# K stationaries copied by ScalarE, full-height masked sums for the tail, and raised priority for norm and GELU in a fused attention and gating kernel

## The chip, the cores and the metric

The kernel runs on one core of one Trainium2 chip. Five engines work side by side, each with its own queue of instructions in a fixed order: TensorE (PE, matmuls, with its weight loads shown as PEld), VectorE (DVE), ScalarE (ACT), GpSimdE (POOL) and SyncE (SP, which here issues the DMAs). The metric is the device time of one execution in microseconds (us). The kernel before takes 469.25 us (median of 3 runs, 469.03 to 470.44).

## The reference, cut to what matters

```python
scores = q @ k.T / 8                      # 4 batches, 12 heads, 448 positions, head size 64
scores = cap * tanh(scores / cap)
attn = exp(scores - max) / (sum + 1e-9)
x = (attn @ v) as [4, 448, 768]
h = gelu_tanh(x @ w_in)                   # w_in [768, 1024]; u, v = two halves of 512
v = layernorm(v) * g_ln
v = w_sg @ v + b_sg                       # w_sg [448, 448], over positions
out = x + (u * v) @ w_out                 # w_out [512, 768]
```

All of it is float32. To reach that accuracy the kernel splits most matmul operands into a high and a low part of type fp32r and adds three products; the attention sums and `attn @ v` are plain fp32 matmuls.

## The kernel before, in words

Heads are taken in pairs: 4 batches of 6 pairs. The 448 positions of k are 3 chunks of 128 and a tail of 64, so each pair has 4 units: three full ones (both heads, scores 128x896) and one tail unit, in which the 64 tail positions of head 0 and of head 1 share the 128 partitions (128x448). In a unit PE makes the scores (`scores`, L198 for the tail and L212 otherwise), ACT applies tanh (`soft`, L225) and exp (`soft2`, L228), and two units later PE multiplies by v (`av`, L241). The pair's q and k are split ahead of time: `prep_a` makes the high part (L156 or L158) and `prep_b` the low part on DVE (L170). For the tail unit the k columns of both heads must stand as one 128-column stationary with zeros between, the tile `kt`; `prep_b` fills it by two copies of 64x128 elements on POOL (L173).

The row sums of exp (`den`, L261) are matmuls of the probabilities with a 0/1 matrix `ones_sb`, 32 output rows each, four of them side by side in one PSUM tile `den`. In batch 0 all four units of a pair go there; in batches 1 to 3 DVE first adds the pair's units up (`presum`, L297). After the sixth pair `recip` inverts the sums (tile `rds`, L322 last); `norm` spreads them by a matmul (L334), multiplies (L337, DVE), makes the high part (L341, ACT) and the low part (L342 and, for the last 64 columns, L344, DVE). Then the gating network of that batch follows: `hv` (L368), `hu` (L412), `vsg` (L426), `outp` (L455, with the residual added in L460). `gelu2` takes four steps in turn: square (L351, ACT), L352 (DVE), tanh (L356, ACT), L357 (DVE).

These matmuls are written between the attention units of the next batch as fillers, at a rate that the code sets (`filler`); the last batch's network runs alone at the end. Beside batch 0 and 1 the weights are loaded and decoded (`decode`, L560 to L582: 36 pieces, ACT or DVE, then DVE, POOL, DVE, ACT or DVE, POOL; `split_sg`, L545 and L546), three or a few more pieces in flight.

The order on each engine is not that of the text: a scheduler at build time picks, among the instructions that are ready in its own plan, the one of highest priority, which is normally the one written first. Once built, an engine's order is fixed.

Of the kernel before, what the change touches and what calls it, by code (L numbers as in the profile page):

```python
# [7 lines left out]
FP32 = mybir.dt.float32  # L8
# [4 lines left out]
ACTF = mybir.ActivationFunctionType  # L13
ALU = mybir.AluOpType
PSUM = bass.MemoryType.PSUM

GELU_A = 0.044715
GELU_C = 0.7978845608028654
# [36 lines left out]
def kernel(  # L55
# [15 lines left out]
    nc = tc.nc  # L71
    B, NP, _, S = q2.shape
    NC = w_sgT.shape[1]
    FC = S // 128
    TL = S - 128 * FC
# [8 lines left out]
    wp = ctx.enter_context(tc.tile_pool(name="wp", bufs=1))  # L84
# [16 lines left out]
    wsg = [wp.tile([128, NC, S], FP32R, name=f"wsg{s}") for s in range(2)]  # L101
    sel_r = wp.tile([128, NP, 128], FP32R, name="sel_r")
    rds = wp.tile([128, S], FP32R, name="rds")
    ones_sb = wp.tile([128, NP + 31], FP32, name="ones_sb")
    bsg_sb = wp.tile([128, S], FP32, name="bsg_sb")
    g_sb = wp.tile([128, KF], FP32, name="g_sb")
    cap_sb = wp.tile([128, 1], FP32, name="cap_sb")
# [3 lines left out]
    kt = wp.tile([128, 2, 2 * TL], FP32R, name="kt")  # L111

    def f32(ap):
        return ap.bitcast(FP32)
# [4 lines left out]
    def later(d, fn):  # L119
        dq.append((now[0] + d, len(dq), fn))  # L120
# [12 lines left out]
    def two(t):  # L133
        return t.rearrange("p (a s) -> p a s", a=2)
# [31 lines left out]
    def prep_b(P):  # L166
        if P >= NPAIR:
            return
        hl = qks[P]
        nc.vector.tensor_tensor(out=hl[:, 1], in0=two(raws[P]), in1=f32(hl[:, 0]), op=ALU.subtract)  # L170
        for h in range(2):
            rows = slice(64 * h, 64 * h + 64)
            nc.gpsimd.tensor_copy(out=kt[rows, :, TL * h:TL * h + TL], in_=f32(hl)[rows, :, 1, 128 * FC:])  # L173
        raw_s.put(raws.pop(P))

    def prep_first():
# [53 lines left out]
    def heads(src, c):  # L230
        if c:
            return [two(src)[:, h, :] for h in range(2)]
        return [src[TL * h:TL * h + TL, :S] for h in range(2)]
# [18 lines left out]
    def den(b, units):  # L252
        if b not in den_t:
            den_t[b] = ps_d.tile([128, 512], FP32, tag="den", name="den")
            units_in[b] = 0
        t = den_t[b]
        for half, (P, c, src) in enumerate(units):
            for h, pr in enumerate(heads(src, c)):
                j = 2 * half + h
                lo, n = (0, 128) if c else (TL * h, TL)  # L260
                nc.tensor.matmul(  # L261
                    out=t[32 * j:32 * j + 32, :S],
                    lhsT=ones_sb[lo:lo + n, NP - 1 - P % NP:NP + 31 - P % NP], rhs=pr,
                    start=(units_in[b] < 2), stop=(units_in[b] >= NP * (NC - ADDS[b]) - 2),
                    skip_group_check=True)
            units_in[b] += 1
# [34 lines left out]
    def flush():  # L301
        b, units = flushes.pop(0)
        den(b, units)
        for u in units:
            raw_s.put(u[2])
        if units_in[b] == NP * (NC - ADDS[b]):
            boost[0] = True
            recip(b)
            later(READY_LAG, set_ready)
# [15 lines left out]
    def gps():  # L325
        if tail[0]:
            tail[0] += 1
            if tail[0] % 2:
                return ps_s.tile([128, 512], FP32, tag="sc", name="gp")
        return ps_g.tile([128, 512], FP32, tag="g", name="gp")  # L330

    def norm(b, p):
        ps = gps()
        yield 1, lambda: nc.tensor.matmul(  # L334
            out=ps[:, :S], lhsT=sel_r[:, p, :], rhs=rds, start=True, stop=True)
        x = xu[:, xu_t[b, p], :]
        nc.vector.tensor_tensor(out=x, in0=x, in1=ps[:, :S], op=ALU.mult)  # L337

        def split():
            xh[p], xl[p] = r_s.get(), r_s.get()  # L340
            nc.scalar.activation(out=xh[p][:, :S], in_=x, func=ACTF.Copy)  # L341
            nc.vector.tensor_tensor(  # L342
                out=xl[p][:, :S], in0=x, in1=f32(xh[p][:, :S]), op=ALU.subtract)
            nc.vector.tensor_tensor(  # L344
                out=xh[p][:, S:], in0=x[:, S - TL:], in1=f32(xh[p][:, S - TL:S]), op=ALU.subtract)
        split()

    def gelu2(src, n, dst, done):
        sqt = t_s.get()
        sq = sqt[:src.shape[0], :n]  # L350
        nc.scalar.activation(out=sq, in_=src, func=ACTF.Square)  # L351
        nc.vector.scalar_tensor_tensor(  # L352
            out=sq, in0=sq, scalar=1.0 / GELU_A, in1=src, op0=ALU.add, op1=ALU.mult)

        def fin():
            nc.scalar.activation(out=sq, in_=sq, func=ACTF.Tanh, scale=GELU_C * GELU_A)  # L356
            nc.vector.scalar_tensor_tensor(  # L357
                out=dst, in0=sq, scalar=1.0, in1=src, op0=ALU.add, op1=ALU.mult)
            t_s.put(sqt)
            done()  # L360
        later(2, fin)
# [307 lines left out]
    for g in range(NSTEP + LAG + 2):  # L669
        P, c = divmod(g, NC)  # L670
# [13 lines left out]
        if g < NSTEP:  # L684
            soft2(g)
            if c == 0:
                prep_a(P + 1)
            elif c == 1:
                prep_b(P + 1)
                load_pair(P + 2)  # L690
# [92 lines left out]
```

## Time and profile before

| what | value |
|---|---|
| median of 3 runs | 469.25 us |
| the profiled execution | 472.69 us, span 470.9 us |
| PE, DVE, ACT, POOL busy | 93%, 71%, 60%, 20% of the span |
| PE idle | nearly all of it before 182 us and after 405 us |
| mean granted TensorE clock | 0.971 of full speed |

The span runs from the first to the last instruction; about 1.8 us lie around it. A group row gives the source line, engine, operation, the tiles written and read, the shapes and the count, then busy us and mean ns of one. "Released by" or "<-" names what ended an engine's idle time.

### The profile page before, as it was taken

The page shows a single profiled execution, that of the slowest core. Times are in us where ns is not written, and L with a number is a line of the kernel's source. Part 1 is how long each engine was busy: PE and PEld are TensorE (multiplying, and loading weights), DVE is VectorE, ACT ScalarE, POOL GpSimd, SP SyncE. Part 2 cuts the span into 40 slices and gives each one's busy share as a digit, 9 for nine tenths or more (in the row PEclk, how much of TensorE's full clock was granted, in tenths as well). Part 3 has the DMA queues.
Part 4 walks back from the last instruction along what each step waited for, and adds up shares of the span by engine and source line. Part 5 has one row for each costly group of instructions (what it writes and reads, how often), then busy time and mean ns, then how long its engine had stood idle before and what let it go on. Part 6 is the DMA issues. An engine that isn't in the chain of part 4 may idle for free.

```text
span 470.9 us, 5916 instructions
## 1 busy us (share of the span) xinstructions
PE 436.7 (93%) x2097; PEld 272.5 (58%) x2097; DVE 335.7 (71%) x621; ACT 283.1 (60%) x420; POOL 93.0 (20%) x143
## 2 busy tenths in 40 slices
PE   5997769879999869999999999999999999899996
PEld 2332223337466536675656666666666576678985
DVE  4859866987999896588587457388596355687662
ACT  4776688974686665538578756636777760044310
POOL 0436644301425543110110101000111000001000
PEclk9999979989999959999999999999999999999999
DMA  7563334221421231231210220420200001200002
GB/s 222 198 197 125 114 120 131 90 84 45 126 67 45 90 107 61 100 99 42 63 39 25 61 61 1 141 91 10 63 22 2 22 2 39 78 1 0 1 27 90
DMA packets 20717, 34.18 MB, mean 73 GB/s; under 512 B 3024, under 2 KB 12880, under 8 KB 20688
## 3 DMA queue, kind: packets, MB, share of 16 engines
q1 hardware_dynamic: 20688, 33.81, 22.8%
q8 instruction: 16, 0.26, 0.3%
q14 instruction: 13, 0.11, 0.1%
HBM read 28.30 MB, written 5.51 MB: 72 GB/s over the span
## 4 chain that ended last, share of the span: by engine, by line
PE 70%; DVE 18%; DMA 3%; POOL 3%; ACT 3%; issue 3%; SPq 0%; POOLq 0%; DVEq 0%; ACTq 0%
PE pav L241 14%; PE gp L455 13%; PE gp L368 11%; PE gp L412 10%; PE sc L212 8%; PE gp L426 8%; DVE raw L297 3%; PE den L261 3%; PE sc L198 2%; DMA xu<-in_w_in_dram 2%; DVE xu L580 2%; PE gp L334 1%; POOL xu L575 1%; ACT raw L225 1%; DVE hl L170 1%
## 5 line engine op out<-in xcount | busy, mean ns | idle before, releaser
L225 ACT ACTIVATE raw<-sc,qsc 128x896 f32<-128x896 f32 (+1 forms) x96 | 86.6, 906 | 36.9 <-PE sc L212 19.1
L241 PE MATMUL pav<-raw,v 128*64 128x448 f32 x384 | 94.1, 576 | 1.0 <-ACT xu L249 1.0
L228 ACT ACTIVATE raw<-raw,cap_sb 128x896 f32<-128x896 f32 (+1 forms) x96 | 90.1, 944 | 1.3
L212 PE MATMUL sc<-hl 64*128 64x448 f32 x432 | 69.6, 418 | 15.0 <-ACT raw L225 15.0
L297 DVE TENSOR_TENSOR raw<-raw,raw 64x448 f32<-64x448 f32 (+1 forms) x72 | 63.2, 878 | 6.1 <-PE pav L241 5.1
L368 PE MATMUL gp<-win,r 128*128 128x512 f32 x264 | 65.3, 398 | 1.3 <-DVE t L357 1.0
L212 PEld LDWEIGHTS sc<-hl 64*128 64x128 f32 x432 | 38.5, 195 | 47.2 <-ACT raw L225 21.5
L412 PE MATMUL gp<-r,win 128*128 128x448 f32 x288 | 65.1, 373 | 0.1
L455 PE MATMUL gp<-r,wout 128*128 128x448 f32 x288 | 63.6, 372 | 0.0
L412 PEld LDWEIGHTS gp<-r,win 128*128 128x128 f32 x288 | 52.7, 188 | 14.5 <-issue 9.6
L455 PEld LDWEIGHTS gp<-r,wout 128*128 128x128 f32 x288 | 53.1, 188 | 11.3 <-issue 3.8
L368 PEld LDWEIGHTS gp<-win,r 128*128 128x128 f32 x264 | 48.2, 188 | 19.5 <-issue 5.6
L241 PEld LDWEIGHTS pav<-raw,v 128*64 128x64 f32 x384 | 25.6, 141 | 52.4 <-issue 41.5
L173 POOL CAST kt<-hl 64x128 fp32r<-64x128 f32 x46 | 21.9, 476 | 155.6 <-PE sc L198 111.3
L426 PE MATMUL gp<-wsg,r 128*128 128x448 f32 x176 | 41.5, 382 | 3.4 <-DVE u L357 3.4
L426 PEld LDWEIGHTS gp<-wsg,r 128*128 128x128 f32 x176 | 33.0, 193 | 14.1 <-issue 6.5
L352 DVE SCALAR_TENSOR_TENSOR t<-t,gp 128x448 f32<-128x448 f32 (+1 forms) x28 | 18.0, 644 | 20.5 <-ACT t L351 20.3
L170 DVE TENSOR_TENSOR hl<-raw,hl 128x896 fp32r<-128x896 f32 x23 | 25.8, 1122 | 8.3 <-ACT hl L158 8.1
L382 POOL TENSOR_TENSOR rs<-rs,pw 128x1 f32<-128x1 f32 (+1 forms) x16 | 9.6, 600 | 109.2 <-DVE rs L381 109.1
L460 DVE TENSOR_TENSOR xu<-xu,gp 128x448 f32<-128x448 f32 x24 | 14.6, 612 | 22.6 <-PE gp L455 22.4
L356 ACT ACTIVATE t<-t 128x448 f32<-128x448 f32 (+2 forms) x32 | 19.3, 604 | 16.9 <-DVE t L352 16.9
L261 PE MATMUL den<-raw,ones_sb 128*32 128x448 f32 (+1 forms) x168 | 29.4, 589 | 0.0
(81 smaller groups left out, 463.7 us busy)
## 6 DMA issues: line engine op xcount, KB each, us to landing
v<-in_vp_dram SPq DMA_DIRECT2D x24, 256.0 KB, 3.0
raw<-in_q_dram SPq DMA_DIRECT2D x24, 224.0 KB, 2.6
raw<-in_k_dram SPq DMA_DIRECT2D x24, 224.0 KB, 3.0
xu<-in_w_in_dram SPq DMA_DIRECT2D x21, 256.0 KB, 2.5
out_dram<-xu SPq DMA_DIRECT2D x24, 224.0 KB, 1.9
raw<-in_w_out_dram SPq DMA_DIRECT2D x11, 256.0 KB, 2.7
u<-in_w_sgT_dram SPq DMA_DIRECT2D x4, 224.0 KB, 5.8
raw<-in_w_in_dram SPq DMA_DIRECT2D x3, 256.0 KB, 3.5
```

The costliest lines, as they stand in the source:

```text
L170: nc.vector.tensor_tensor(out=hl[:, 1], in0=two(raws[P]), in1=f32(hl[:, 0]), op=ALU.subtract)
L173: nc.gpsimd.tensor_copy(out=kt[rows, :, TL * h:TL * h + TL], in_=f32(hl)[rows, :, 1, 128 * FC:])
L212: nc.tensor.matmul(out=sc[:, h, :S], lhsT=hl[rows, w, 1, 128 * c - 128:128 * c], rhs=hl[rows, m, 0], start=(i == 0), stop=(i == 2))
L225: nc.scalar.activation(out=prob(g), in_=src, func=ACTF.Tanh, scale=qsc)
L228: nc.scalar.activation(out=prob(g), in_=prob(g), func=ACTF.Exp, scale=cap_sb)
L241: nc.tensor.matmul(out=pav_t[P][64 * h:64 * h + 64, :S], lhsT=w, rhs=two(p_t[g])[:, h if c else 0, :], start=(g % NC == 0), stop=(c == NC ...
L261: nc.tensor.matmul(out=t[32 * j:32 * j + 32, :S], lhsT=ones_sb[lo:lo + n, NP - 1 - P % NP:NP + 31 - P % NP], rhs=pr, start=(units_in[b] < ...
L297: eng.tensor_tensor(out=a, in0=a, in1=w, op=ALU.add)
L368: yield 1, lambda i=i, c=c, a=a, w=w: nc.tensor.matmul(out=ps, lhsT=a[c][:, t * 128:t * 128 + 128], rhs=win[w][:, c, HF:], start=(i == 0), ...
L412: yield 1, lambda a=a, w=w, c=c, st=st, sp=sp: nc.tensor.matmul(out=ps, lhsT=win[w][:, c, f * 128:(f + 1) * 128], rhs=a[c][:, :S], start=s ...
L426: yield 1, lambda i=i, c=c, a=a, w=w: nc.tensor.matmul(out=ps, lhsT=a[c][:, f * 128:(f + 1) * 128], rhs=wsg[w][:, c, :], start=(i == 0), s ...
L455: yield 1, lambda ps=ps, c=c, a=a, w=w, f=f, st=st, sp=sp: nc.tensor.matmul(out=ps, lhsT=wout[w][:, f, c * 128:(c + 1) * 128], rhs=a[f][:, ...
```

## The change

The 46 copies into `kt` go from POOL to ACT. The tail's sum matmuls take all 128 partitions, with a stationary that is zero for the other head's 64 rows, in place of 64 partitions each; `ones_sb` becomes three matrices. The operations of `norm` and of `gelu2` are put into a block of high priority, which the scheduler takes ahead of other ready work.

```diff
-    ones_sb = wp.tile([128, NP + 31], FP32, name="ones_sb")
+    ones_sb = wp.tile([128, 3, NP + 31], FP32, name="ones_sb")
...
-            nc.gpsimd.tensor_copy(out=kt[rows, :, TL * h:TL * h + TL], in_=f32(hl)[rows, :, 1, 128 * FC:])
+            nc.scalar.activation(
+                out=kt[rows, :, TL * h:TL * h + TL], in_=f32(hl)[rows, :, 1, 128 * FC:], func=ACTF.Copy)
...
-            for h, pr in enumerate(heads(src, c)):
+            for h in range(2):
                 j = 2 * half + h
-                lo, n = (0, 128) if c else (TL * h, TL)
                 nc.tensor.matmul(
                     out=t[32 * j:32 * j + 32, :S],
-                    lhsT=ones_sb[lo:lo + n, NP - 1 - P % NP:NP + 31 - P % NP], rhs=pr,
+                    lhsT=ones_sb[:, 0 if c else 1 + h, NP - 1 - P % NP:NP + 31 - P % NP],
+                    rhs=two(src)[:, h if c else 0, :],
...
-        nc.vector.tensor_tensor(out=x, in0=x, in1=ps[:, :S], op=ALU.mult)
+        with tc.high_priority():
+            nc.vector.tensor_tensor(out=x, in0=x, in1=ps[:, :S], op=ALU.mult)
...
-        split()
+        with tc.high_priority():
+            split()
...
-        nc.scalar.activation(out=sq, in_=src, func=ACTF.Square)
-        nc.vector.scalar_tensor_tensor(
-            out=sq, in0=sq, scalar=1.0 / GELU_A, in1=src, op0=ALU.add, op1=ALU.mult)
+        with tc.high_priority():
+            nc.scalar.activation(out=sq, in_=src, func=ACTF.Square)
+            nc.vector.scalar_tensor_tensor(
+                out=sq, in0=sq, scalar=1.0 / GELU_A, in1=src, op0=ALU.add, op1=ALU.mult)
...
-            nc.scalar.activation(out=sq, in_=sq, func=ACTF.Tanh, scale=GELU_C * GELU_A)
-            nc.vector.scalar_tensor_tensor(
-                out=dst, in0=sq, scalar=1.0, in1=src, op0=ALU.add, op1=ALU.mult)
+            with tc.high_priority():
+                nc.scalar.activation(out=sq, in_=sq, func=ACTF.Tanh, scale=GELU_C * GELU_A)
+                nc.vector.scalar_tensor_tensor(
+                    out=dst, in0=sq, scalar=1.0, in1=src, op0=ALU.add, op1=ALU.mult)
...
+    for h in range(2):
+        ones[TL * h:TL * h + TL, 1 + h, NP - 1::NP] = 1.0
```

The lines below the edits move by one to nine (the tanh L225 becomes L226, the exp L228 becomes L229, `norm`'s L337, L342 and L344 become L339, L344 and L346, `gelu2`'s L352 and L357 become L356 and L362, `decode`'s L563 to L580 become L568 to L585).

ACT around the tail unit of a pair of batch 0, before (`raw_73` is the tail's probability tile, `win_117` a decoded weight piece):

```order
L225 ACTIVATE raw_73<-sc,qsc 128x448
L158 ACTIVATE win_117<-xu 128x256
L228 ACTIVATE raw_73<-raw_73,cap_sb 128x448
L225 ACTIVATE raw_75<-sc,qsc 128x896
L563 ACTIVATE xu<-xu 128x256
L228 ACTIVATE raw_75<-raw_75,cap_sb 128x896
```

The same place after the change:

```order
L226 ACTIVATE raw_73<-sc,qsc 128x448
L173 ACTIVATE kt<-hl 64x2x64
L229 ACTIVATE raw_73<-raw_73,cap_sb 128x448
L173 ACTIVATE kt<-hl 64x2x64
L226 ACTIVATE raw_75<-sc,qsc 128x896
```

The two copies into `kt` now stand on either side of the tail's exp, and the decode's cast has moved elsewhere.

DVE at the norm of batch 0, behind the last step of the inverted sums, before (`xu` are the attention outputs, `r_...` their high and low parts):

```order
L322 TENSOR_TENSOR rds<-t_102,rds 64x448
L297 TENSOR_TENSOR raw_77<-raw_77,raw_70 128x896
L337 TENSOR_TENSOR xu<-xu,gp 128x448 x2
L580 TENSOR_TENSOR raw_72<-raw_72 128x256
L337 TENSOR_TENSOR xu<-xu,gp 128x448
L342 TENSOR_TENSOR r_80<-xu,r_79 128x448
L344 TENSOR_TENSOR r_79<-xu,r_79 128x64
L342 TENSOR_TENSOR r_82<-xu,r_81 128x448
L344 TENSOR_TENSOR r_81<-xu,r_81 128x64
```

The same place after the change:

```order
L323 TENSOR_TENSOR rds<-t_102,rds 64x448
L298 TENSOR_TENSOR raw_77<-raw_77,raw_70 128x896
L339 TENSOR_TENSOR xu<-xu,gp 128x448 x4
L344 TENSOR_TENSOR r_80<-xu,r_79 128x448
L339 TENSOR_TENSOR xu<-xu,gp 128x448 x2
L344 TENSOR_TENSOR r_82<-xu,r_81 128x448
L344 TENSOR_TENSOR r_86<-xu,r_85 128x448
```

All six multiplications and the low parts now follow each other, and the decode step and the 64-column pieces come later.

DVE at the GELU of the last `hu` block of batch 0, before (`t_103` is its temporary, `raw_67` a weight piece in decode, `raw_73` a running sum of `presum`):

```order
L297 TENSOR_TENSOR raw_73<-raw_73,raw_72 64x448 x2
L580 TENSOR_TENSOR raw_74<-raw_74 128x256
L297 TENSOR_TENSOR raw_73<-raw_73,raw_76 128x896
L352 SCALAR_TENSOR_TENSOR t_103<-t_103,gp 128x448
L565 TENSOR_SCALAR raw_67<-raw_67 128x256
L297 TENSOR_TENSOR raw_73<-raw_73,raw_69 128x896
L357 SCALAR_TENSOR_TENSOR u_101<-t_103,gp 128x448
```

The same place after the change:

```order
L298 TENSOR_TENSOR raw_73<-raw_73,raw_72 64x448 x2
L585 TENSOR_TENSOR raw_77<-raw_77 128x256
L570 TENSOR_SCALAR raw_74<-raw_74 128x256
L170 TENSOR_TENSOR hl<-raw_75,hl 128x896
L356 SCALAR_TENSOR_TENSOR t_103<-t_103,gp 128x448
L572 TENSOR_SCALAR raw_74<-raw_74 128x256
L570 TENSOR_SCALAR raw_67<-raw_67 128x256
L440 SCALAR_TENSOR_TENSOR t_104<-gp,g_sb,bsg_sb 128x448
L362 SCALAR_TENSOR_TENSOR u_101<-t_103,gp 128x448
```

The two large additions of `presum` (128x896) no longer stand ahead of and between the two DVE steps of this GELU.

## Rows read from the trace of the kernel before

**Rows 1.** The page's head.

```profile
span 470.9 us, 5916 instructions
```

**Rows 2.** Windows: stretch, its us, busy (count) by engine, PEclk, DMA share, GB/s.

```profile
12.00:96.00 84.00, 69.02 (x361) 25.38 (x357) 65.06 (x138) 64.72 (x98) 38.99 (x58) 0.94 0.42 138
96.00:108.00 12.00, 11.36 (x33) 4.38 (x34) 10.03 (x22) 7.48 (x15) 0.73 (x1) 0.86 0.21 71
108.00:160.00 52.00, 50.92 (x250) 33.41 (x250) 47.90 (x103) 36.72 (x60) 20.72 (x28) 1.00 0.29 84
160.00:182.00 22.00, 15.21 (x52) 8.66 (x51) 17.59 (x37) 11.42 (x21) 9.97 (x13) 0.69 0.28 84
182.00:405.00 223.00, 223.00 (x1103) 145.43 (x1104) 147.28 (x232) 139.67 (x192) 19.28 (x33) 1.00 0.15 49
405.00:471.00 66.00, 60.49 (x282) 52.02 (x280) 42.80 (x79) 17.90 (x31) 2.19 (x4) 1.00 0.08 31
```

**Rows 3.** Timeline of PE, two sum groups: start, us, engine, line, form.

```profile
75.26 0.96 PE L261 MATMUL den<-raw,ones_sb 128*32 128x448 f32 x8
...
79.41 1.82 PE L261 MATMUL den<-raw,ones_sb 128*32 128x448 f32 x8
```

**Rows 4.** Groups by line and form: the sum matmuls.

```profile
L261 PE MATMUL den<-raw,ones_sb 128*32 128x448 f32 x144 | 23.4, 585 | 0.0
L261 PE MATMUL den<-raw,ones_sb 64*32 64x448 f32 x24 | 6.4, 615 | 0.0
```

**Rows 5.** The chain that ended last: start, us, what.

```profile
17.12 1.75 PE den L261 x8
...
68.53 3.27 PE den L261 x8
```

**Rows 6.** Groups by line: the copies, and the nearest forms on ACT.

```profile
L173 POOL CAST kt<-hl 64x128 fp32r<-64x128 f32 x46 | 21.9, 476 | 155.6 <-PE sc L198 111.3 <-DVE hl L170 20.9 <-DVE xu L460 15.5
...
L158 ACT ACTIVATE win<-xu 128x256 fp32r<-128x256 f32 x11 | 4.6, 415 | 6.8 <-DVE xu L580 6.8
...
L660 ACT ACTIVATE guard<-guard 128x1 f32<-128x1 f32 x1 | 0.2, 192 | 0.0
```

**Rows 7.** Windows of L173 alone, columns as in rows 2 for POOL.

```profile
0.00:96.00 96.00, 5.72 (x16) 0.95 0.47 148
96.00:182.00 86.00, 3.62 (x8) 0.90 0.28 82
```

**Rows 8.** Timeline: low part of the next pair and the tail's tanh, batch 0.

```profile
54.63 1.08 DVE L170 TENSOR_TENSOR hl<-raw,hl 128x896 fp32r<-128x896 f32 x1
...
55.99 0.61 ACT L225 ACTIVATE raw<-sc,qsc 128x448 f32<-128x448 f32 x1
```

**Rows 9.** Timeline: from the inverted sums of batch 0 to its `hv`.

```profile
95.96 0.62 DVE L322 TENSOR_TENSOR rds<-t,rds 64x448 fp32r<-64x448 f32 x1
...
106.55 0.62 DVE L337 TENSOR_TENSOR xu<-xu,gp 128x448 f32<-128x448 f32 x1
...
107.74 10.27 PE L368 MATMUL gp<-win,r 128*128 128x512 f32 x44
```

**Rows 10.** Waits in the stretch 160 to 182 us: total, times, longest.

```profile
PE sc L212 <- ACT raw L225: 3.4, 1, 3.4
PE gp L426 <- DVE u L357: 3.4, 1, 3.4
```

**Rows 11.** Timeline: the GELU of the last `hu` block of batch 0.

```profile
166.84 0.52 ACT L351 ACTIVATE t<-gp 128x448 f32<-128x448 f32 x1
...
171.81 0.61 DVE L357 SCALAR_TENSOR_TENSOR u<-t,gp 128x448 f32<-128x448 f32 x1
```

**Rows 12.** Timeline: norm of the last batch, at the end of the program.

```profile
411.26 1.69 DVE L337 TENSOR_TENSOR xu<-xu,gp 128x448 f32<-128x448 f32 x3 [0.56 <-PE gp L334]
...
413.09 11.14 PE L368 MATMUL gp<-win,r 128*128 128x512 f32 x46 [0.15 <-ACT r L341]
...
419.29 0.60 ACT L351 ACTIVATE t<-gp 128x512 f32<-128x512 f32 x1 [2.12 <-PE gp L368]
```

More of the change, by code (lines that the diff above doesn't have):

```diff
@@ L748 @@
         w_sgT[:128 * FC].reshape(FC, 128, S).transpose(1, 0, 2), _np.concatenate([tail, tail])[:, None]], axis=1)
-    ones = _np.zeros((128, NP + 31), _np.float32)
-    ones[:, NP - 1::NP] = 1.0
+    ones = _np.zeros((128, 3, NP + 31), _np.float32)
+    ones[:, 0, NP - 1::NP] = 1.0
+    for h in range(2):
+        ones[TL * h:TL * h + TL, 1 + h, NP - 1::NP] = 1.0
     sel = _np.zeros((2, 2, 32, NP, 2, D), _np.float32)
```

## The prediction

> **What bounds the kernel now.** I read the windows by stage first. From 182 to 405 us PE is busy 223.00 of 223.00 us at the full clock; before it, PE is idle 15.0 us from 12 to 96, 0.6 to 108, 1.1 to 160 and 6.8 to 182; behind it 5.5 us [rows 2]. Of the span of 470.9 us [rows 1] some 30 us can therefore be won by better order, nearly all before 182 us, where batch 0 and the first gating network share the engines with the weight decode. Nothing is to be had from 182 to 405 us: the matmuls there stay the same.
>
> Which engine paces the first 182 us? From 12 to 96 us DVE works 65.06 and ACT 64.72 of 84 us, PE 69.02: none is full, they wait for each other in fixed order. From 96 to 160 us DVE works 57.93 of 64 us (10.03 + 47.90), so there it is nearly full, and from 160 to 182 us 17.59 of 22 while PE stands still for 6.8 us [rows 2]. The reader is to see two kinds of stretch: one of chains (12 to 96), one where DVE has only 6.1 us to spare (96 to 160). Then the waits: in 160 to 182 us PE has two stalls of 3.4 us, one for ACT's tanh, one for the last step of a GELU on DVE [rows 10]. [...]
>
> **Part 1, masked tail sums.** A group of eight sum matmuls in batch 0 takes 0.96 us without a tail unit and 1.82 us with one [rows 3]: 0.86 us more. The 24 records on 64 rows are six such groups (4 records per tail unit, 24 / 4 = 6) [rows 4], all in batch 0. With 128-row matmuls all groups should look like the first: 6 x 0.86 = 5.2 us of PE. On the path are those in the chain, two: 1.75 us, and 3.27 us where the clock was low [rows 5]. They save about half each, 0.86 + 1.6 = 2.5 us. The other four lie beside ACT and DVE work, which hides them; without that cover all 5.2 us would count. Bounds 0 and -5.2 (-6 with the slow group); I take -2.5.
>
> [...] The rows first: the matmuls on 64 rows last 615 ns on average, those on 128 rows 585 ns [rows 4], so fewer rows are no faster. [...]
>
> **Part 2, the copies on ACT.** 46 copies of 476 ns leave POOL [rows 6]. On ACT their form isn't in the trace: 128x256 takes 415 ns and 128x1 192 ns [rows 6], so 128 elements lie between, by interpolation about 0.30 us. Two per pair are 0.6 us, 46 x 0.30 = 13.8 us in all, 3% of the span. From 182 us on ACT works 139.67 of 223 us [rows 2]; the 11 pairs there (23 - 12) x 0.6 = 6.6 us vanish in its 83 us of idle time, and PE has units in hand. Before 182 us there are 12 pairs (24 copies), 8 of them up to 96 us [rows 7]. There ACT is 77% busy (64.72 / 84); were all of it on the path, it would cost 12 x 0.6 = +7.2 us, were it all hidden 0. I take 40% of the first eight pairs, 8 x 0.6 x 0.4 = +1.9 us, since beyond 96 us it is DVE that is full.
>
> The new wait is ACT's for the low part (L170). What is queued behind it on ACT is the tail's exp, behind the second copy the next unit's tanh, and for these wait PE's `av` and next scores. In the order shown the first copy stands after the tail's tanh. In the trace the low part ends at 55.71 us (54.63 + 1.08) and that tanh at 56.60 us (55.99 + 0.61): 0.9 us to spare [rows 8]. It holds, but not by much; the price of missing it is in the rivals. On POOL the copies stood ahead of decode steps; 5.72 us of POOL's 40 us up to 96 us go (38.99 from 12 us on and little before) [rows 2], [rows 7]. POOL is under half busy, so I count only -0.7 us (bounds 0 and -5.7). The larger `ones_sb` transfer (128x111 in place of 128x37 words, 38 KB more) stands on SP's queue ahead of the second pair's load; its first use is behind 17 us [rows 5]: nothing.
>
> **Part 3, priority of norm.** In batch 0 the inverted sums are there at 96.6 us (95.96 + 0.62), the last multiplication (L337) ends at 107.2, and `hv` starts at 107.74: 11.1 us of norm, with decode and attention between [rows 9]. In the new DVE order four multiplications and one low part follow each other: 5 x 0.62 = 3.1 us after the first matmul, so `hv` could start near 101 by DVE. On PE the six norm matmuls, eight `av` and three tail scores still stand ahead; seven score matmuls that stood there now come behind. I put `hv` at 102 to 104, 4 to 6 us sooner. But what is jumped over has to be done: it lands in the stretch to 160 us, where DVE has 6.1 us to spare for all (64 - 57.93) [rows 2]. Bounds 0 and -6.1; I take -2.5, a bit under half.
>
> The same at the end of the program is a wash, and it can be worked out. There all six multiplications now precede the first low part: 411.26 + 6 x 0.56 (1.69 / 3) = 414.6, + 0.62 = 415.2. `hv` has done two matmuls by then and needs 16 more for its first block, 16 x 0.242 (11.14 / 46) = 3.9: 419.1 us. In the trace the block's GELU starts at 419.29 [rows 12]: it waits today for the second half of the multiplications instead. Zero, with 1 us either way. Norms of batches 1 and 2 lie inside the stretch where PE is full: zero.
>
> **Part 4, priority of GELU.** In the stall that ends near 172 us the GELU takes from 166.84 to 172.42 (171.81 + 0.61), of which its four steps work some 2.4 us (0.52, 0.61 and two taken as alike); 3 us is queueing, on DVE behind large additions and decode steps [rows 11]. In the new order those large additions are out of the way, though the low part (1.08 us) [rows 8] still stands ahead. The stall of 3.4 us for it should shrink to 1 or less; the one for tanh is decode steps on ACT waiting for DVE, and shrinks only if those come sooner. Together -2.5 us. [...]
>
> **The sum.** -2.5 + 1.9 - 0.7 - 2.5 - 2.5 = -6.3 us, on an execution of 472.69 us (span 470.9, 1.8 us around it). That one lies 3.4 us above the median of the runs; the terms are too small for the scale to matter: 469.25 - 6.3 = 462.95, so 463.
>
> **Rivals.** *DVE is the bound from 96 to 182 us.* It works 75.5 of 86 us there (10.03 + 47.90 + 17.59) [rows 2] and the change gives it nothing less to do; priority only changes who waits. Then parts 3 and 4 give 0, part 1's gain and the copies nearly cancel: -2.5 + 1.9 - 0.7 = -1.3, 468 to 470 us. Against it: 10 us of its idle time are there, and the stalls are of its making.
>
> *ACT becomes the bound, slower.* Place: the copies in the pairs before 182 us. Price: 12 x 0.6 = 7.2 us, and where a copy reaches ACT before the low part is done, up to 1.1 us more per pair; nine or ten such pairs at half of it make 5 us. With -2.5 from the tail sums and -5 from parts 3 and 4: 469.25 + 7.2 + 5 - 7.5 = 474. It decides from the point where ACT is over 95% busy between 12 and 96 us, or where its wait for L170 passes 0.5 us per pair. For it: 0.9 us to spare [rows 8]. Against it: 19 us of idle ACT there (84 - 64.72).
>
> [...]
>
> *The tail sums gain nothing*, since the new form could be held up elsewhere: 463 + 2.5 = 465.5. It stays in the forecast's range.
>
> **How the numbers follow.** Forecast (457.5 to 467.5, the last rival in it) 0.55; DVE bound 0.15; ACT bound 0.15; all stalls gone 0.15. Three runs spread over 0.3%, so 1.4 us is about what can be told from no change. Faster by more: 0.55 + 0.15 + 0.03 of the DVE case = 0.73; within: 0.12; slower: 0.15. The time is the forecast's, 463. For the range I go down to 453, which takes in most of the last case, and up to 473, which takes in the DVE case and half of the ACT case.
>
> **What would show it.** Right: every group of eight sums near 0.96 us; 46 ACT copies near 0.30 us with little idle time ahead of them; `hv` of batch 0 starting some 6 us after `rds`; no wait of PE on the GELU's last step near 170 us, and the low clock there shorter; 182 to 405 us unchanged in length. Wrong: ACT waiting for L170; PE idle before the last `hu` and `vsg` as long as now; or the time of the middle stage changed, which no step here foresees.

## The result, and the profile after

| | median of runs | to before on the same chip |
|---|---|---|
| changed kernel, first measurement (4 runs) | 464.87 us | ratio 0.9886, 95% interval 0.9843 to 0.9929 |
| changed kernel, second measurement (12 runs) | 465.25 us | ratio 0.9913, 95% interval 0.9882 to 0.9944 |

It is faster by 4 to 5 us. The sum forecast 463.0, so the total was nearly right; most of its terms were not, and this is what the rest is about.

First the head of the page and the windows by stage of the changed kernel; they answer to [rows 1, 2] with the same columns (PE, PEld, DVE, ACT, POOL, clock, DMA share, GB/s).

```profile
span 463.1 us, 5890 instructions
```

```profile
12.00:96.00 84.00, 73.04 (x387) 28.01 (x384) 65.90 (x139) 71.54 (x115) 32.97 (x38) 0.94 0.44 143
96.00:108.00 12.00, 10.40 (x46) 7.28 (x45) 8.13 (x24) 6.03 (x13) 8.75 (x7) 1.00 0.14 44
108.00:160.00 52.00, 47.62 (x229) 30.08 (x228) 47.93 (x106) 38.60 (x68) 18.93 (x23) 0.97 0.28 84
160.00:182.00 22.00, 16.15 (x72) 10.35 (x69) 19.60 (x38) 14.97 (x26) 10.68 (x10) 0.84 0.26 79
```

PE does 4.0 us more in 12 to 96 us than before (73.04 against 69.02) and 4.3 us less in 96 to 160 (58.02 against 62.28): a gain early, a loss behind it. Starts and ends read from the trace show where. Four stretches of the span: up to the inverted sums of batch 0, from there to the first `hv` matmul, from that to the first `outp` matmul, and the rest.

| kernel | to inverted sums | to `hv` | `hv` to `outp` | rest | span |
|---|---|---|---|---|---|
| before | 96.6 | 11.1 | 80.0 | 283.2 | 470.9 |
| changed | 88.9 | 6.4 | 85.7 | 282.1 | 463.1 |
| changed, second profile | 87.9 | 6.6 | 84.6 | 282.4 | 461.5 |

The rest is the same within 1.1 us, as foreseen. Ahead of `hv` 12.4 us are gained (7.7 + 4.7), and 5.7 are given back between `hv` and `outp`. One profile is one execution: before and two kernels below that have its order on PE (e9, e11) reach the inverted sums at 96.6, 93.5 and 93.5 us, so differences under 3 us are not read from such a table. In e9 and e11 `hv` starts at 103.0 us (before: 107.7); against these two the gain ahead of `hv` is 7.7 us.

What are the 4.7 us? The stretch from the inverted sums to `hv`, and that from `hv` to the first `hu` matmul, before and then changed:

```profile
96.58:107.73 11.15, 11.09 (x32) 4.12 (x32) 9.21 (x21) 6.63 (x13) 0.73 (x1) 0.85 0.20 66
107.74:130.26 22.52, 21.50 (x97) 14.65 (x97) 19.53 (x42) 14.30 (x24) 7.95 (x11) 1.00 0.31 90
```

```profile
88.87:95.28 6.41, 6.28 (x21) 2.23 (x21) 4.92 (x8) 4.69 (x8) 0.00 (x0) 1.00 0.23 72
95.29:125.38 30.09, 25.08 (x107) 15.91 (x106) 24.42 (x60) 18.11 (x33) 15.07 (x16) 0.96 0.18 54
```

Before, PE was busy for 11.09 of the 11.15 us ahead of `hv`, so there was no idle time to win. It does 21 matmuls there now in place of 32, and its clock was 0.85 in the one execution and 1.00 in the other. The attention matmuls that `hv` overtook come behind its start: up to `hu` PE works 3.6 us more (25.08 against 21.50). Only the rest of that stretch's growth, 4.0 us, is idle time (5.0 against 1.0).

The sum matmuls by form answer to [rows 4], and the copies to [rows 6]:

```profile
L261 PE MATMUL den<-raw,ones_sb 128*32 128x448 f32 x168 | 25.6, 570 | 3.5 <-DVE raw L298 3.5
L173 ACT ACTIVATE kt<-hl 64x128 fp32r<-64x128 f32 x46 | 14.0, 303 | 1.6 <-DVE hl L170 1.1
```

And three groups of eight sums in a row, of which every second holds a tail unit [rows 3]:

```profile
66.64 0.96 PE L261 MATMUL den<-raw,ones_sb 128*32 128x448 f32 x8
71.52 0.96 PE L261 MATMUL den<-raw,ones_sb 128*32 128x448 f32 x8
75.48 0.96 PE L261 MATMUL den<-raw,ones_sb 128*32 128x448 f32 x8
```

All three take 0.96 us, where the mixed group took 1.82. A copy on ACT takes 303 ns, and in the whole program ACT waits 1.1 us for the low part.

Where do the 5.0 idle us come from? PE's timeline through `hv` of the changed kernel (start, us, line, form; in brackets the idle time before, and who ended it):

```profile
95.29 7.82 PE L373 MATMUL gp<-win,r 128*128 128x512 f32 x33
...
107.29 2.11 PE L373 MATMUL gp<-win,r 128*128 128x512 f32 x8 [1.60 <-DVE t L362]
...
113.57 0.50 PE L373 MATMUL gp<-win,r 128*128 128x512 f32 x1 [0.84 <-DVE t L362]
...
122.02 0.94 PE L261 MATMUL den<-raw,ones_sb 128*32 128x448 f32 x4 [2.57 <-DVE raw L298]
...
125.38 2.28 PE L417 MATMUL gp<-r,win 128*128 128x448 f32 x8
```

PE waits for the GELU's last step and for DVE's partial sums, 5.0 us in three stalls. DVE's timeline a little ahead of them:

```profile
101.28 0.69 DVE L356 SCALAR_TENSOR_TENSOR t<-t,gp 128x512 f32<-128x512 f32 x1 [0.32 <-ACT t L355]
105.48 0.43 DVE L585 TENSOR_TENSOR xu<-xu 128x256 f32<-128x256 f32 x1 [3.52 <-POOL xu L580]
...
106.56 0.67 DVE L362 SCALAR_TENSOR_TENSOR t<-t,gp 128x512 f32<-128x512 f32 x1
```

DVE stands for 3.52 us in front of a decode addition (L585) that waits for POOL's multiplication (L580), and the GELU's last step (L362) is queued behind it. POOL's timeline:

```profile
98.32 5.88 POOL L551 TENSOR_TENSOR wsg<-u,wsg 128x448 fp32r<-128x448 f32 x3 [9.93 <-ACT wsg L550]
104.15 0.73 POOL L587 TENSOR_TENSOR win<-raw,win 128x256 fp32r<-128x256 f32 x1
104.83 0.62 POOL L580 TENSOR_TENSOR xu<-xu 128x256 f32<-128x256 f32 x1
```

Three of the four subtractions that make the low parts of the gating weights (`wsg`, `split_sg`) stand there in one block; before they ran one at a time at 36.7 to 76.5 us. No line of the diff touches them: with the copies moved from POOL to ACT, the scheduler put them elsewhere. It did so on ACT too. The high parts of the same pieces (L550), for the first of which POOL stands 9.93 us, now come behind the norm; before, the four ran one at a time at 34.3 to 75.1 us:

```profile
97.68 0.56 ACT L550 ACTIVATE wsg<-u 128x448 fp32r<-128x448 f32 x1
98.71 1.03 ACT L550 ACTIVATE wsg<-u 128x448 fp32r<-128x448 f32 x2
```

Last, the waits of PE from 150 to 184 us, which answer to [rows 10]:

```profile
PE gp L431 <- DVE t L440: 5.9, 1, 5.9
PE den L261 <- DVE raw L298: 1.0, 1, 1.0
```

In place of the two stalls of 3.4 us stands one of 5.9 us, and PE waits in it for a step of `vsg` on DVE (L440), no longer for the GELU's last step.

### The profile page after: what moved, and what is told of

Read it like the earlier page. It is cut to its first block, busy times and chain, and to the rows that moved or that the text cites. A ratio compares the mean times of both kernels' runs of the same rounds, so it can differ in the third digit from the quotient of the medians.

```text
span 463.1 us, 5890 instructions
## 1 busy us (share of the span) xinstructions
PE 429.2 (93%) x2097; PEld 271.4 (59%) x2097; DVE 332.5 (72%) x621; ACT 293.1 (63%) x466; POOL 80.1 (17%) x97
## 4 chain that ended last, share of the span: by engine, by line
PE 69%; DVE 16%; DMA 4%; ACT 4%; issue 3%; POOL 3%; SPq 0%; DVEq 0%; POOLq 0%; ACTq 0%
PE gp L460 13%; PE pav L242 12%; PE gp L417 11%; PE gp L373 10%; PE sc L213 9%; PE gp L431 8%; DMA xu<-in_w_in_dram 3%; PE den L261 2%; DVE raw L298 2%; PE sc L199 2%; ACT raw L226 2%; DVE hl L170 1%; DVE xu L585 1%; PE gp L335 1%; DVE xu L339 1%
## 5 line engine op out<-in xcount | busy, mean ns | idle before, releaser
L226 ACT ACTIVATE raw<-sc,qsc 128x896 f32<-128x896 f32 (+1 forms) x96 | 86.8, 907 | 40.5 <-PE sc L199 19.9
L242 PE MATMUL pav<-raw,v 128*64 128x448 f32 x384 | 91.0, 574 | 2.1 <-ACT xu L250 2.1
L229 ACT ACTIVATE raw<-raw,cap_sb 128x896 f32<-128x896 f32 (+1 forms) x96 | 90.0, 943 | 0.8
L213 PE MATMUL sc<-hl 64*128 64x448 f32 x432 | 68.4, 415 | 9.1 <-ACT raw L226 9.1
L373 PE MATMUL gp<-win,r 128*128 128x512 f32 x264 | 66.8, 402 | 2.9 <-DVE t L362 2.4
L373 PEld LDWEIGHTS gp<-win,r 128*128 128x128 f32 x264 | 48.3, 189 | 22.5 <-issue 7.5
L170 DVE TENSOR_TENSOR hl<-raw,hl 128x896 fp32r<-128x896 f32 x23 | 26.4, 1149 | 7.7 <-ACT hl L158 7.6
L361 ACT ACTIVATE t<-t 128x448 f32<-128x448 f32 (+2 forms) x32 | 19.3, 603 | 18.3 <-DVE t L356 18.2
L356 DVE SCALAR_TENSOR_TENSOR t<-t,gp 128x448 f32<-128x448 f32 (+1 forms) x28 | 18.1, 645 | 16.2 <-ACT t L355 16.0
L261 PE MATMUL den<-raw,ones_sb 128*32 128x448 f32 x168 | 25.6, 570 | 3.5 <-DVE raw L298 3.5
L580 POOL TENSOR_TENSOR xu<-xu 128x256 f32<-128x256 f32 x22 | 17.4, 793 | 37.3 <-DVE xu L578 17.6
```

The source lines that it names most:

```text
L213: nc.tensor.matmul(out=sc[:, h, :S], lhsT=hl[rows, w, 1, 128 * c - 128:128 * c], rhs=hl[rows, m, 0], start=(i == 0), stop=(i == 2))
L226: nc.scalar.activation(out=prob(g), in_=src, func=ACTF.Tanh, scale=qsc)
L229: nc.scalar.activation(out=prob(g), in_=prob(g), func=ACTF.Exp, scale=cap_sb)
L242: nc.tensor.matmul(out=pav_t[P][64 * h:64 * h + 64, :S], lhsT=w, rhs=two(p_t[g])[:, h if c else 0, :], start=(g % NC == 0), stop=(c == NC ...
L261: nc.tensor.matmul(out=t[32 * j:32 * j + 32, :S], lhsT=ones_sb[:, 0 if c else 1 + h, NP - 1 - P % NP:NP + 31 - P % NP], rhs=two(src)[:, h ...
L373: yield 1, lambda i=i, c=c, a=a, w=w: nc.tensor.matmul(out=ps, lhsT=a[c][:, t * 128:t * 128 + 128], rhs=win[w][:, c, HF:], start=(i == 0), ...
```

## The experiments

All are timed in five rounds against before. The ratio compares with before on the same chips; 0.001 is 0.47 us.

| run | edit | median us | ratio, 95% interval |
|---|---|---|---|
| e4_k_only | before + copies on ACT (larger `ones_sb` too) | 468.38 | 0.9979 (0.9950 to 1.0008) |
| e9_d_only | before + masked tail sums | 468.47 | 0.9965 (0.9942 to 0.9988) |
| e10_prio_only | before + both priorities (larger `ones_sb` too) | 468.23 | 0.9969 (0.9947 to 0.9992) |
| e1_k_off | changed, copies on POOL | 466.00 | 0.9942 (0.9913 to 0.9971) |
| e2_d_off | changed, 64-row tail sums | 467.05 | 0.9957 (0.9922 to 0.9993) |
| e3_p_off | changed, no priorities | 466.34 | 0.9944 (0.9916 to 0.9971) |
| e6_norm_off | changed, no norm priority | 466.11 | 0.9935 (0.9909 to 0.9961) |
| e7_gelu_off | changed, no GELU priority | 465.27 | 0.9912 (0.9886 to 0.9937) |
| e8_changed_again | changed | 465.25 | 0.9913 (0.9882 to 0.9944) |
| e5_wsg_dve | changed, `wsg` low parts on DVE | 460.11 | 0.9815 (0.9766 to 0.9863) |
| e12_wsg_dve_prio_off | e5 without priorities | 463.72 | 0.9869 (0.9836 to 0.9901) |
| e11_before_wsg_dve | before, `wsg` low parts on DVE | 469.19 | 0.9986 (0.9962 to 1.0010) |

The stretches of their profiles, as in the table above (e2's profiled execution, 472.1 us, was the slowest of its twelve and is left out):

| | to inverted sums | to `hv` | `hv` to `outp` | rest |
|---|---|---|---|---|
| copies on POOL: e1, e9, e10 | 94.0, 93.5, 94.3 | 6.7, 9.5, 8.2 | 80.7, 78.4, 81.0 | 282.4, 283.0, 282.3 |
| before with `wsg` on DVE: e11 | 93.5 | 9.6 | 78.5 | 284.4 |
| copies on ACT: e3, e4, e7 | 88.0, 91.7, 88.8 | 9.6, 9.6, 6.4 | 84.8, 84.3, 85.7 | 282.8, 282.7, 282.2 |
| copies on ACT: e6 | 89.6 | 9.9 | 81.7 | 284.0 |
| copies on ACT, `wsg` on DVE: e5, e12 | 87.3, 90.1 | 6.4, 9.5 | 79.3, 78.7 | 283.8, 285.0 |

**The copies.** e1 undoes this part in the changed kernel, e4 does it alone:

```diff
-            nc.scalar.activation(
-                out=kt[rows, :, TL * h:TL * h + TL], in_=f32(hl)[rows, :, 1, 128 * FC:], func=ACTF.Copy)
+            nc.gpsimd.tensor_copy(out=kt[rows, :, TL * h:TL * h + TL], in_=f32(hl)[rows, :, 1, 128 * FC:])
```

> The changed kernel with the k copies back on POOL; masked tail sums and both priorities stay. In the trace of the changed kernel the attention of batch 0 is already 8 us ahead of before at 55 us, where neither norm nor GELU has run; so either the copies' move or the tail sums put it there. Theory (the copies' move makes that gain, by fewer decode steps being put ahead of attention on DVE): the lead at 55 us falls to 0 to 2 us, the inverted sums of batch 0 come at about 95 us instead of 88.9, and the time is 466 to 469 us. Rival A (tail sums make the lead): nothing changes before 96 us, and without 24 small ACT copies ahead of 182 us the time is 463 to 465. Rival B (the prediction's own sizes: copies cost +1.9, relief of POOL -0.7): 1 us faster than the changed kernel, 463 to 464.

> The kernel before with the copies on ACT as the only edit; tail sums on 64 rows, no priorities. Theory (the move of the copies makes the lead in batch 0 by the order of the decode steps): inverted sums of batch 0 at about 91 us instead of 96.6; of these 5 to 6 us the full DVE behind takes half back: 466 to 468 us, 2 to 3 us faster than before. Rival A (tail sums make the lead): 470 to 471, as predicted by +1.9 - 0.7. Rival B (ACT becomes the bound by the copies): 474 or more, ACT waiting for the low part.

The early lead is theirs: the 91st score matmul starts at 48.8 to 54.1 us in all kernels with the copies on ACT (53.4 in e4), at 58.3 to 60.6 in those with the copies on POOL (58.5 in e1). The time is another matter: e1 is only 0.29% (1.4 us) behind the changed kernel, e4 0.21% (1.0 us) ahead of before, neither beyond its interval; e4 missed the 2 to 3 us that were expected. The table shows what becomes of the lead: with the copies on ACT and `wsg` on POOL the inverted sums come 2 to 6 us sooner (88.0 to 91.7 against 93.5 to 94.3; the latest is e4, the one without masked sums), and in all but e6 the stretch from `hv` to `outp` is 84 to 86 us in place of 78 to 81. The four `wsg` subtractions in e1 and e4 (ns min/median/max, first and last start):

```profile
L550 POOL TENSOR_TENSOR wsg<-u,wsg x4: 1137/1166/1332, 35.6 to 73.6; 128x448 fp32r<-128x448 f32 x4
```

```profile
L547 POOL TENSOR_TENSOR wsg<-u,wsg x4: 1151/1242/3462, 48.0 to 107.4; 128x448 fp32r<-128x448 f32 x4
```

So the copies' move alone, without any priority, puts the block behind the norm. Rival A of both expectations (tail sums make the early lead) and the rival that ACT becomes the bound (474) are out.

**The tail sums.** e2 undoes them, e9 does them alone; in e9 the order of instructions is that of before, in e2 that of the changed kernel.

```diff
-                    lhsT=ones_sb[:, 0 if c else 1 + h, NP - 1 - P % NP:NP + 31 - P % NP],
-                    rhs=two(src)[:, h if c else 0, :],
+                    lhsT=ones_sb[lo:lo + n, 0, NP - 1 - P % NP:NP + 31 - P % NP], rhs=pr,
```

> The changed kernel with the tail units summed by matmuls on 64 rows again; the rest stays. The order of all instructions on DVE and PE is that of the changed kernel, so this shows the price of the form alone. Theory (as predicted, about half of 6 x 0.86 us on the path): 467 us, 1.5 to 3 us slower than the changed kernel, the inverted sums of batch 0 at about 91 us instead of 88.9. Rival A (tail sums make the whole lead of 8 us at 55 us): inverted sums at 96 us, time 468 to 470. Rival B (all of it lies beside other work): the time of the changed kernel within 1 us, 464 to 466.

> The kernel before with the masked tail sums as the only edit (tail units summed by 128-row matmuls); copies on POOL, no priorities; the order on every engine stays that of before. Theory (the form saves about half of 6 x 0.86 us alone, and the rest of the gain in batch 0 needs the copies' move): inverted sums of batch 0 at 94 us instead of 96.6, time 1.5 to 2.5 us under before. Rival (alone they gain nothing, since each group waits for ACT and DVE anyway): within 1 us of before. Rival (they alone make the changed kernel's lead): inverted sums at 90 us, 4 us under before.

e9 is 0.35% (1.6 us) faster than before, e2 0.44% (2.1 us) slower than the changed kernel. Some 2 us either way, near the predicted 2.5, and with an unchanged order it is the form itself. e1 and e10 share one order too and differ by this form alone: 1.3 us (0.9942 against 0.9969). Taken singly, only e9's gain is beyond its interval. In e2 the form's price is seen again:

```profile
L262 PE MATMUL den<-raw,ones_sb 128*32 128x448 f32 x144 | 26.2, 574 | 4.8 <-DVE raw L298 4.8
L262 PE MATMUL den<-raw,ones_sb 64*32 64x448 f32 x24 | 6.4, 615 | 0.0
```

The sums take 32.6 us here (26.2 + 6.4) against 25.6; this is e2's slowest execution, so only the forms are read from it: 64 rows are again no faster than 128.

**The priorities.** e3 removes both blocks of `tc.high_priority()` from the changed kernel, e6 that of `norm`, e7 that of `gelu2`; e10 adds both to before.

```diff
-        with tc.high_priority():
-            nc.vector.tensor_tensor(out=x, in0=x, in1=ps[:, :S], op=ALU.mult)
+        nc.vector.tensor_tensor(out=x, in0=x, in1=ps[:, :S], op=ALU.mult)
...
-        with tc.high_priority():
-            nc.scalar.activation(out=sq, in_=src, func=ACTF.Square)
+        nc.scalar.activation(out=sq, in_=src, func=ACTF.Square)
```

> The changed kernel without the priorities of norm and GELU; copies on ACT and masked sums stay. Theory (the lead up to the inverted sums is not due to priority; priority adds 4 us at the norm, half of which is taken back while DVE is full from 96 to 160 us, and some 2 us at the stall near 170 us): inverted sums still at about 89 us, hv of batch 0 at about 100 us instead of 95.3, the PE stall ahead of hu's GELU near 165 us back at about 3 us, the time 466 to 468. Rival A (DVE is the bound from 96 to 182 us, priority only changes who waits): hv later but the end the same, 464 to 466. Rival B (priority gives nearly all): 469 to 470.

> The changed kernel without the priority of norm; that of GELU stays. Theory: from the inverted sums of batch 0 to hv 9.6 us instead of 6.4, as in the variant without both; of these 3.2 us half is lost by the end: 1 to 2 us slower than the changed kernel, 466 to 467. Rival (GELU's priority is worth nothing, norm's is worth all): as the variant without both. Rival (DVE full behind hv takes all of it): as the changed kernel.

> The changed kernel without the priority of GELU; that of norm stays. Theory (as predicted, -2.5 of a stall near 170 us): the stall of PE before the last hu GELU comes back with 2 to 3 us; 466 to 467, 1 to 2 us slower than the changed kernel. Rival (the copies and norm have already moved the large additions away, GELU's priority changes only who waits): within 1 us of the changed kernel.

> The kernel before with the priorities of norm and GELU as the only edit. The low parts of wsg run early on POOL here, so nothing blocks DVE behind the norm. Theory (priority is worth its 3 to 4 us at the norm where no POOL block gives it back): hv of batch 0 some 7 us behind the inverted sums instead of 11.1, time 2 to 4 us under before. Rival (DVE full from 96 to 160 us takes all of it back): within 1 us of before.

e7 has the changed kernel's time to 0.02 us (465.27 against 465.25): GELU's priority is worth nothing. Norm's takes 3 us out of the stretch to `hv` (9.6 to 9.9 us without, 6.4 with), but e6 is only 1.0 us behind by ratio, within the intervals. e10 missed the 2 to 4 us that were expected of it; by ratio it is 1.5 us faster than before. It has no block on POOL, and `hv` starts 8.2 us behind the inverted sums (9.5 in e9 and e11), but `hu` comes 25.6 us behind `hv` in place of 22.5:

```profile
102.54:128.16 25.62, 24.71 (x109) 15.33 (x107) 24.43 (x57) 15.65 (x27) 8.36 (x12) 1.00 0.26 78
```

PE is idle for 0.9 us there, about as before (1.0); it does 109 matmuls in place of 97. So norm's lead is handed back without any wait, as attention work that `hv` had overtaken. The stall near 165 us, which GELU's priority was to shorten, is 5.8 to 5.9 us with or without it (e7, then e3):

```profile
PE gp L429 <- DVE t L438: 5.8, 1, 5.8
```

```profile
PE gp L427 <- DVE t L436: 5.9, 1, 5.9
```

In e1, with the copies on POOL and the priorities on, the two stalls are those of before, 3.4 us for L361 (the GELU's last step) and 2.9 for tanh:

```profile
PE gp L430 <- DVE u L361: 3.4, 1, 3.4
PE sc L212 <- ACT raw L225: 2.9, 1, 2.9
```

The expectation for e7, a stall that comes back, missed: a stall of that length had never gone. e8, the changed kernel again, stood beside them:

> The changed kernel itself, unchanged, on the chip of these runs, as the base of the three others: 464 to 466 us.

**The block on POOL.** e5 moves the `wsg` low parts of the changed kernel to DVE; PE's order stays the same word for word. e11 does the same to before, and e12 removes the priorities from e5.

```diff
-            nc.gpsimd.tensor_tensor(
+            nc.vector.tensor_tensor(
                 out=wsg[1][:, c, :], in0=t, in1=f32(wsg[0][:, c, :]), op=ALU.subtract)
```

> The changed kernel with the low parts of the gating weights (wsg, four subtractions of 128x448) on DVE in place of POOL; PE's order stays the same. In the trace of the changed kernel three of them fill POOL from 98.3 to 104.2 us, a decode step behind them on POOL ends at 105.4, and DVE waits 3.5 us for it, with the GELU and the partial sums of hv behind; in the variant with the copies on POOL these subtractions ran at 35 to 74 us and that wait is absent. Theory (this POOL block is what hands the lead of hv back): DVE's wait of 3.5 us goes, hv to hu takes 26 to 27 us instead of 30.1, and the time is 1 to 3 us under the changed kernel: 462 to 464. Rival (DVE is full there whatever POOL does, and gets 4 x 0.6 = 2.4 us more): hv to hu stays at 29 to 31 us, time as the changed kernel or 1 us above.

> The kernel before with the four low parts of wsg on DVE in place of POOL, as a control for the 5 us that the same edit took from the changed kernel. Theory (those 5 us come from the block of three on POOL at 98 to 104 us, which before doesn't have: there they run at 36 to 76 us): within 1.5 us of before, to either side. Rival (POOL's share in these subtractions is slow anywhere, and any kernel gains by it): 3 to 5 us under before.

> The changed kernel with wsg's low parts on DVE and without both priorities. With the POOL block in place, taking the priorities away cost 1 us. Theory (the block gave the norm's 3.2 us back): without the block the priorities are worth their full size, so this is 3 us slower than the variant with wsg on DVE and priorities (460.1): 462.5 to 464. Rival (the priorities are worth 1 us whatever stands on POOL): 461 to 462.

e5 takes 460.11 us, 5.1 us under the changed kernel on the same chip, more than the 1 to 3 us expected, and the best of all. e11 stays within 1 us of before (interval across 1): the gain isn't POOL's slowness as such, it needs the order that the change makes. The subtractions in e5 now run apart from one another:

```profile
L551 DVE TENSOR_TENSOR wsg<-u,wsg x4: 586/608/1161, 48.2 to 129.6; 128x448 fp32r<-128x448 f32 x4
```

PE in e5, where the two GELU stalls in `hv` are gone, `hu` starts 26.9 us behind `hv` (30.1 in the changed kernel), and the stall near 165 us is down to 1.32:

```profile
117.13 0.99 PE L261 MATMUL den<-raw,ones_sb 128*32 128x448 f32 x4 [2.26 <-DVE raw L298]
...
120.62 2.12 PE L417 MATMUL gp<-r,win 128*128 128x448 f32 x8
...
160.26 1.68 PE L431 MATMUL gp<-wsg,r 128*128 128x448 f32 x7 [1.32 <-DVE t L440]
```

The 3.2 us in `hv` are what the theory said. But `hu` then lasts 3.0 us longer (34.2 against 31.2), with three of the four subtractions on DVE in it (120.8 to 129.6 us), and the stretch from `vsg` to `outp` shrinks by 6.3 (24.4 to 18.1). That second gain was not expected. The order on DVE and ACT changed too. DVE in the changed kernel, then in e5:

```profile
163.08 1.61 DVE L170 TENSOR_TENSOR hl<-raw,hl 128x896 fp32r<-128x896 f32 x1
164.61 0.61 DVE L356 SCALAR_TENSOR_TENSOR t<-t,gp 128x448 f32<-128x448 f32 x1
...
165.55 0.67 DVE L440 SCALAR_TENSOR_TENSOR t<-gp,g_sb,bsg_sb 128x448 f32<-128x448 f32 x1
```

```profile
157.44 0.60 DVE L356 SCALAR_TENSOR_TENSOR t<-t,gp 128x448 f32<-128x448 f32 x1
...
159.54 0.67 DVE L440 SCALAR_TENSOR_TENSOR t<-gp,g_sb,bsg_sb 128x448 f32<-128x448 f32 x1
...
161.51 1.08 DVE L170 TENSOR_TENSOR hl<-raw,hl 128x896 fp32r<-128x896 f32 x1
```

In e5 GELU's first DVE step (L356) and the `vsg` step (L440), for which PE waits, stand ahead of the next pair's low part (L170); in the changed kernel behind it and behind decode. How much of the 5.1 us is POOL's block and how much this new order can't be told apart by these runs, since one edit makes both.

e12 is 3.6 us behind e5 by medians, 2.5 by ratios (0.9869 against 0.9815), measured against before on different occasions. With the block in place the same priorities were worth 1.1 us by medians and 1.5 by ratios (e3). By itself this would speak for the theory that the block gave norm's gain back. But the intervals overlap, e12's profile is already 2.8 us behind e5's at the inverted sums (90.1 against 87.3), ahead of the first norm, and in e10, without the block, the priorities are worth 1.5 us as well. So the theory isn't shown.

## Why the prediction was right in total and wrong in its parts

By ratios, with each part taken away from the changed kernel and each put alone into before (intervals of about 0.25 to 0.35% on each, so 1.2 to 1.7 us):

| part | predicted | taken away | alone |
|---|---|---|---|
| tail sums | -2.5 | -2.1 | -1.6 |
| copies (+1.9 - 0.7) | +1.2 | -1.4 | -1.0 |
| norm priority | -2.5 | -1.0 | -1.5 |
| GELU priority | -2.5 | 0.0 | (with norm) |
| sum | -6.3 | -4.5 | -4.1 |

That the total came near is luck in part: the copies came out 2 to 3 us better than forecast, the two priorities 3 to 4 us worse.

**Tail sums: right, in the form's price and the size.** The groups take 0.96 us (one, at 60.6 us with a granted clock of 0.50, 1.72; the slow group of before, 3.27 us in [rows 5], had 0.50 as well), PE's time in the sums falls from 29.4 us (both forms of [rows 4], overlap counted once) to 25.6, and to 24.2 in e9, where 5.2 was reckoned, and 1.6 to 2.1 us of it arrive. The 64-row form cost time although its matmuls read half the partitions: 615 ns on average against 574 on 128 rows in e2, and 1.82 us against 0.96 for a group that holds a tail unit [rows 3]. What makes the mixed group dear, no run here shows.

**Copies: the instruction was priced right and the term was too dear.** 0.30 us was interpolated, 303 ns measured; the low part was not missed (1.1 us of waiting in all). ACT from 12 to 96 us rose by 6.8 us (64.72 to 71.54; 4.8 of copies were reckoned) and had room. The +1.2 lies outside e4's interval, which ends at +0.4 us; that the copies gain, by 1.0 to 1.4, is likely and not clear of noise. What failed is the step "by POOL relief of -0.7 us": it priced the 46 instructions and took the rest of the order as given. The scheduler made another order with them gone. Before, the second to eighth low parts (L170) had 0, 3, 6, 11, 14, 17 and 18 decoded weight pieces ahead of them on DVE, now 1, 3, 6, 9, 12, 15 and 17; attention came sooner, and three `wsg` subtractions, due only at `vsg`, slid behind the norm with their casts on ACT, where they held up decode, GELU and `hv`. The kernel's order showed this in POOL's queue, three rows on end, and the prediction looked only at places in ACT's and DVE's. Whether the early lead is due to that order or to a freer POOL, and whether the block came of POOL's relief or of ACT's new work, was not tried apart and stays open.

**Norm priority: the order came as predicted, its price was wrong.** `hv` starts 6.4 us behind the inverted sums, "some 6 us" as predicted, 4.7 sooner than before. What failed is the bound: -6.1 was DVE's spare time, while PE was idle for only 0.6 us from 96 to 108 and 1.1 us to 160 [rows 2], and up to `hv` not at all (11.09 of 11.15 us busy). `hv` changed places with attention matmuls, and some of the 11.1 us went with a low clock: six `av` matmuls from 97.68 us on took 2.86 us at a granted 0.59, six from 104.39 us on took 1.72 at 1.00. e9 and e11, in the same order, take 9.5 and 9.6 us to `hv`. That part of the lead would be given back between 96 and 160 us was predicted, and put down to DVE being full. e10 gives it back with no wait of PE. In the changed kernel a wait comes on top: DVE was as full as before from 108 to 160 us (47.93 against 47.90 us), but ahead of that, from 96 to 108, it did only 8.13 of 12 us (10.03 before): it was waiting, for POOL. What the 1.0 to 1.5 us measured are made of stays open.

**GELU priority: wrong.** The stall near 170 us was read as queueing on DVE behind work that GELU could jump over. In the changed kernel the GELU's first DVE step starts at 164.61, right behind a low part of 1.61 us, with the priority on; the time is the same without it. The wait for the GELU's last step went, as predicted, but PE's idle time from 160 to 182 us fell only from 6.8 to 5.9 us, with `vsg`'s step (L440) standing behind the same low part. The clock did rise, from 0.69 to 0.84 in 160 to 182 us. In e5 the same window has PE busy nearly throughout and the full clock:

```profile
160.00:182.00 22.00, 21.39 (x104) 14.08 (x104) 21.46 (x41) 16.42 (x30) 8.21 (x10) 1.00 0.24 68
```

**End of the program: a wash, as worked out.** Norm of the last batch in the changed kernel, which answers to [rows 12] (DVE, PE, ACT):

```profile
403.19 3.28 DVE L339 TENSOR_TENSOR xu<-xu,gp 128x448 f32<-128x448 f32 x6 [0.56 <-PE gp L335]
```

```profile
412.15 0.60 ACT L355 ACTIVATE t<-gp 128x512 f32<-128x512 f32 x1 [5.07 <-PE gp L373]
```

From the first multiplication to the first GELU it takes 8.96 us, before 8.03 (419.29 - 411.26): 0.9 later, within the 1 us given.

Of the rivals, "DVE is the bound" was near on the priorities (0 against 1.1 to 1.5 us measured for both) and wrong on the copies; "ACT becomes the bound" did not come; the case of all stalls gone (0.15, and the lower end of the range with it) needed the edit of e5, which at 460 us comes part of the way, with PE idle for 0.6 us (22 - 21.39) from 160 to 182 us at a clock of 1.00. What the clock of 0.69 there cost before, no run shows by itself.

## What to carry to other kernels

Moving instructions from one engine to another under a scheduler changes more than these instructions: compare the order of every engine, the relieved one and the one that took the work above all, and look for work not touched by the change that now stands in a block ahead of something urgent. A gain early in a program is worth what is left of it at the next full stretch, so follow a lead from stage to stage before counting it. Before pricing a priority, read the idle time of the engine that bounds the stage: an instruction that only changes places with other work on a busy engine has gained nothing yet. And when several small terms add up to the right total, test each alone: here one was too dear by 2 to 3 us and one was nothing.

## What was not expected of the hardware

The first `wsg` subtraction of the block on POOL took three times as long as the two behind it, all of 128x448 elements; in all seven profiles with the block it took 3.45 to 3.65 us, the two behind it 1.14 to 1.16:

```profile
98.32 3.65 POOL L551 TENSOR_TENSOR wsg<-u,wsg 128x448 fp32r<-128x448 f32 x1 [9.93 <-ACT wsg L550]
...
101.93 1.16 POOL L551 TENSOR_TENSOR wsg<-u,wsg 128x448 fp32r<-128x448 f32 x1
...
103.04 1.15 POOL L551 TENSOR_TENSOR wsg<-u,wsg 128x448 fp32r<-128x448 f32 x1
```

The windows over the two parts of the block show what DVE did beside them:

```profile
98.30:101.97 3.67, 3.67 (x18) 3.05 (x17) 3.35 (x14) 2.35 (x5) 3.65 (x2) 1.00 0.22 71
101.97:104.20 2.23, 2.23 (x12) 1.27 (x12) 0.00 (x0) 0.63 (x1) 2.23 (x3) 1.00 0.00 0
```

While DVE was busy 3.35 of 3.67 us, the subtraction took 3.65 us; with DVE idle 1.15. It started inside a run of short DVE instructions, and these kept their pace: the addition L585 of 128x256 took 0.42 us.

A busy DVE alone does not make POOL slow, though. Before, all four subtractions ran beside a DVE that was busy for over 90% of their time, and took 1.13 to 1.33 us. There the DVE instructions that started just behind them were the slow ones, with 1.24, 1.34, 1.56 and 1.35 us; the second and the last are the same addition, which took 0.42 above:

```profile
48.54 1.14 POOL L546 TENSOR_TENSOR wsg<-u,wsg 128x448 fp32r<-128x448 f32 x1
48.61 1.34 DVE L580 TENSOR_TENSOR xu<-xu 128x256 f32<-128x256 f32 x1 [0.78 <-POOL xu L575]
```

So in the changed kernel DVE was at work first and kept its pace, and POOL took three times as long (3.65 us against 1.15). Before, at 48.54 and at 76.52 us, POOL was at work first and kept its pace (1.14 and 1.13 us), and DVE's addition took three times as long (1.34 and 1.35 us against 0.42). What makes the one slow beside the other, no run here shows. On DVE itself the same subtraction takes 0.61 us (median in e5). The POOL instruction that started inside a run of DVE work was dear here: 3.65 us, and behind its block DVE waited 3.52 us for POOL.
